# More products of zeros, the first loads at once, and a new order of work in a fused attention and MoE kernel

## The chip, the cores and the metric

The kernel runs on one core of one Trainium2 chip. The metric is the device time of one execution in microseconds (us). TensorE (PE in the rows) multiplies matrices, VectorE (DVE) and ScalarE (ACT) do elementwise work, GpSimd (POOL) does a little of it, and SyncE (SP) issues nearly all transfers (DMA).

## The reference

Linear attention, a norm, and a two-layer network with the activation h·cos(h), all in float32:

```python
kv  = einsum('bhsd,bhse->bhde', k, v)          # 8 batches, 8 heads, 576 tokens, 64 columns
out = einsum('bhsd,bhde->bhse', q, kv)
x   = out / sqrt(mean(out*out, -1) + 1e-6) * g_norm      # heads side by side: 4608 x 512
h   = x @ w_in                                 # 512 -> 2048
y   = (h * cos(h)) @ w_out                     # 2048 -> 512
```

## The kernel before

**Tiling.** The 4608 tokens are nine chunks of 512. The width of 2048 is sixteen blocks of 128, with a weight tile `wi` and a weight tile `wo` for each. A step is one chunk and one block. Its first stage makes h in a PSUM bank, from four groups of three products of 512 columns (`xhi` with two parts of `wi`, `xlo` with one). ScalarE and VectorE make h·cos(h) from it (`ki`, `r`, then `ghi` and `glo`), and its second stage adds it onto four `acc` tiles with four groups of three products. The products of 128 x 512 are nearly all of TensorE's work.

**The front.** The first two chunks (`FRONT`) are made ready in another way than the later ones. For each of four pairs of heads p, `kv_front_part` multiplies k and v of a batch (36 small products for batch 0, 24 for batch 1), and `x_front_part` transposes q (four products with `ident`), multiplies it with kv, takes the norm, and transposes back (four products, `ident` and `r`). Their tiles are lent from buffers that later hold weights, so k, v and q of the front stand in the rows under names such as `wo` and `wi`. The last of the front's k and v are those of batch 1, p = 3.

**Weights.** They come as 64-bit words of 512 KB a tile. `w_part` turns them into two float32r parts, with some three operations on ScalarE and four on VectorE.

**The order of work.** The program holds a small planner (`Order`). Each piece of work is a generator that asks for an engine, a duration and a priority. The planner puts the pieces on the engines by its own estimates, and the instructions are issued in that order and kept in it. `due(i)` is the planned time of step i, `haste` adds a correction to the priority of single pieces (through `put_off`), and loads are pieces on a planned engine "DMA". So a changed number moves instructions on all engines. Loads of weights are issued on line 437, the front's k and v on 386 and 388, its q on 418 and 423, all from SP; the first k and v come from ScalarE's queue. Line 207 is the helper through which every compute instruction goes.

**The start.** 34 products of zeros run on TensorE while the first loads are on their way.

Of the kernel before, what the change touches and what calls it, by code (L numbers as in the profile page):

```python
# [15 lines left out]
AF = mybir.ActivationFunctionType  # L16
# [35 lines left out]
class Order:  # L52
# [23 lines left out]
    def advance(self, proc, value):  # L76
        while True:
            try:
                req = proc.gen.send(value)
            except StopIteration:  # L80
                self.live.discard(proc)
                return
            value = None
            self.seq += 1
            if req[0] == "run":
                proc.shape = req[3] if len(req) > 3 else None
                self.pending.append((req[2], self.seq, proc.t, req[1], proc))
                return
            if req[0] == "wait":
                proc.t = max([proc.t] + [e.t for e in req[1] if e.t is not None])  # L90
                proc.left = [e for e in req[1] if e.t is None]
                if proc.left:
                    for e in proc.left:
                        e.waiters.append(proc)
                    return
            else:
                tokens = req[1]
                if not tokens.free:
                    heapq.heappush(tokens.waiters, (req[2] if len(req) > 2 else -100.0, self.seq, proc))
                    return  # L100
                t, value = heapq.heappop(tokens.free)
                proc.t = max(proc.t, t)
# [24 lines left out]
    def run(self):  # L127
        while self.pending:
# [15 lines left out]
            if e == "PE":  # L144

                d = (2 * d if start < 6 else d) + (self.CHANGE if proc.shape != self.shape else 0)
                self.shape = proc.shape
# [7 lines left out]
def tile_kernel(  # L155
# [40 lines left out]
    sched = Order()  # L196
    sched.busy["DMA"] = 1.0

# [40 lines left out]
    bank = ps_s.tile([P, 512], F32, name="bank0")  # L239
    for _ in range(34):  # L240
        pe.matmul(out=bank[:, 0:P], lhsT=zeros, rhs=zeros, start=True, stop=True)
    ident = const.tile([P, P], F32, name="ident")
# [26 lines left out]
    def due(i):  # L269
# [4 lines left out]
    haste = {  # L274
        ("load kv", 0, 0): -15.1, ("load kv", 0, 1): 6.2, ("load kv", 0, 2): 2.5, ("load kv", 0, 3): 3.5,
        ("load kv", 1, 1): -98.4, ("load kv", 1, 3): 27.5, ("load q", 0, 0): -4.0, ("load q", 0, 1): -28.8,
        ("load q", 0, 3): -16.6, ("load q", 1, 0): -10.5, ("load q", 1, 2): 10.0, ("load q", 1, 3): -24.8,
        ("load", "wi", 3): 10.0, ("load", "wo", 0): 10.0, ("load", "wo", 1): -130.0, ("load", "wo", 2): -13.1,
        ("kv", 0, 1): -13.1, ("kv", 0, 3): -10.0, ("x", 1, 0): -90.9, ("x", 1, 1): -5.1, ("x", 1, 2): -20.0,
        ("x", 1, 3): 11.8, ("wi", 1): 10.0, ("wi", 12): 8.7, ("wi", 13): 5.0, ("wi", 7): -10, ("wi", 9): -5,  # L280
        ("wo", 0): -46.3, ("wo", 12): 19.2, ("wo", 13): 59.3, ("wo", 2): 10.6, ("wo", 4): 10.6, ("wo", 5): -7.5,
        ("wo", 8): 14.1, ("h", 10): -14.4, ("h", 11): 75.5, ("h", 13): 6.2, ("h", 15): -21.9, ("h", 23): 16.3,
        ("h", 26): -21.2, ("h", 31): 25.1, ("h", 36): 54.9, ("h", 4): 10, ("act", 11): -46.1, ("act", 13): 15.3,
        ("act", 16): 16.2, ("act", 29): 32.0, ("act", 35): 63.7, ("act", 4): -10, ("act", 5): -8.1,
        ("act", 8): 10.6, ("acc", 0): 28.7, ("acc", 1): 19.9, ("acc", 10): 20.7, ("acc", 13): 59.2,
        ("acc", 14): 44.4, ("acc", 18): 32.3, ("acc", 26): 10.6, ("acc", 28): 15.6, ("acc", 33): 25.2,
        ("acc", 46): 5.6, ("acc", 53): 6.8, ("acc", 8): 12.3, ("xd", 2, 0): -3.8, ("xd", 2, 2): -11.8,
        ("xd", 2, 3): -24.5, ("xd", 3, 0): -12.5,
    }
# [31 lines left out]
    kv_split = {(b, p): Event() for b in range(FRONT) if max(chunks_of(b)) >= FRONT for p in range(NP)}  # L321
    g_in, over_in = Event(), events(B)
    w_done = {key: Event() for key in need}
# [26 lines left out]

    def load_g():
        pass

    def g_part():
        yield "wait", [g_in]
        yield "run", [("ACT", 0.1)], -11.0
        act.copy(out=gcol[D:2 * D, :], in_=gcol[0:D, :])

    def two(shape, dtype, which):
# [16 lines left out]
    def kv_loads_front(b, p, tags):  # L376

        def issue():
            shape = [P, 2, SQ, D] if b else [P, SF, D]
            kv_tiles[b, p] = [wpool.tile(shape, F32, name=f"{kind}{j}") for kind, j in tags]  # L380
            for t, src in zip(kv_tiles[b, p], (k, v)):
                heads = src[b, 2 * p:2 * p + 2]

                queue = nc.sync if b or p else act
                if b:
                    queue.dma_start(out=t[0:SP], in_=heads.rearrange("h (p i) d -> p h i d", i=SQ))  # L386
                else:
                    queue.dma_start(out=t, in_=heads.rearrange("h (p i) d -> (h p) i d", i=SF))
            if not b and not p:
                act.activation(out=warm, in_=warm, func=AF.Sin)  # L390
                act.dma_start(out=gcol[0:D, :], in_=g_norm.rearrange("(d o) -> d o", o=1))
        return issue
# [59 lines left out]
    def kv_front_part(b, p, prio):  # L452
# [13 lines left out]
        sched.fire(kv_used[b, p], end)  # L466
        done = [Event(), Event()]

        def copies(j):
# [61 lines left out]
    def x_front_part(c, p, prio):  # L531
# [5 lines left out]
        qn = q_tiles.pop((c, p)).rearrange("p j (m s) d -> p (j m) (s d)", s=2)  # L537
        ps_t = ps_tile(bank)
        for n in range(NTT):
            pe.transpose(out=ps_t[:, n * P:(n + 1) * P], in_=qn[:, n, :], identity=ident)  # L540
# [4 lines left out]
        give_ps(bank, end)  # L545
        todo = front_rows(c)
        yield "wait", [kv_done[b, p] for b in {b for b, _, _, _ in todo}]
        acc = (p + 2) % NTT
# [22 lines left out]
        def heads(t):  # L571
# [7 lines left out]
        dve.tensor_scalar(out=ms, in0=ms, scalar1=EPS, scalar2=None, op0=ALU.add)  # L579
        yield "run", [("POOL", 1.4)], prio  # L580
        rinv = small.tile([P, 2 * NTT], F32, name="rinv")
# [5 lines left out]
            out=heads(x), in0=heads(ps[:, 0:CH]),  # L587
            in1=rinv.rearrange("p (n o) -> p n o", o=1).broadcast_to([P, 2 * NTT, D]), op=ALU.mult)
        _, end = yield "run", [("PE", 0.5)], prio
        for a in range(NTT):  # L590
# [20 lines left out]
    def x_part(c, p, prio):  # L611
# [20 lines left out]
        for j in range(2):  # L632
            yield "take", t_psa, prio
            banks.append((yield "take", t_bank, prio))
        _, end = yield "run", [("PE", sum(2 * max(0.11, (n + 32) / 2400) for _, _, _, n in parts))], -1.0
        both = [ps_tile(bank) for bank in banks]
# [61 lines left out]
    def w_part(key, prio):  # L698
# [22 lines left out]
        act.activation(out=w32, in_=words(F32, 1), func=AF.Copy, scale=HW_SCALE)  # L721
        yield "wait", [low_done]
        yield "run", [("DVE", 0.69)], prio
        wi = w32.bitcast(I32)
# [52 lines left out]
    def act_part(i, h, bank):  # L777
# [10 lines left out]
        dve.scalar_tensor_tensor(out=r, in0=ki, scalar=-C2, in1=r, op0=ALU.mult, op1=ALU.add)  # L788
        sched.give(t_ki, end)

        yield "run", [("ACT", act_us())], prio
# [21 lines left out]
    def stage2_part():  # L813
        for i, (c, j, first, final) in enumerate(steps):
            yield "wait", [w_done["wo", j], g_done[i]]
            for t in range(NTT):
# [13 lines left out]
                if final:  # L830
                    sched.spawn(out_part(c, t, accs[t], j == NJ - 1, due(i + 3)), end + 0.1)
            sched.give(t_g, end)
# [63 lines left out]
    for b in range(FRONT):  # L896
        used = [q_used[c, p] for c in range(FRONT) if c >= b for p in range(NP)]
        used += [e for (x, _), e in kv_split.items() if x == b]
        [(kind, j)] = lend(1, used, -1)
        kv_front.append(wpool.tile([P, H, P], F32, name=f"{kind}{j}"))  # L900
        (pool if b else dve).memset(kv_front[b], 0.0)
    for c in range(FRONT):
        for p in range(NP):
            t = due(begin[c]) - 32 + 3 * p if c else -100.0 + p
            t += put_off("load kv", c, p)
            load(2.4 if c else 1.9, t, [kv_in[c, p]], kv_loads_front(c, p, lend(2, [kv_used[c, p]])))
            if p in (0, 2):
                [key] = lend(1, [q_used[c, p], q_used[c, p + 1]])
            t += put_off("load q", c, p)
            load(1.1 if c else 0.85, t, [q_in[c, p]], q_loads_front(c, p, key))  # L910
            if c == 0 and p == 1:
                load(0.5, t, [g_in], load_g)
                sched.spawn(g_part())
    for c in range(FRONT):
# [4 lines left out]
    for key in sorted(need, key=lambda x: (need[x], x)):  # L919
        t = due(need[key]) - 14.0 + put_off("load", *key)  # L920
        load(1.5, t, [w_in[key]], w_loads(key), wait=lent.get(key, ()))
        sched.spawn(w_part(key, due(need[key]) - 0.0 + put_off(*key)))
# [58 lines left out]
```

## Time and profile before

| | |
|---|---|
| time, median of 3 runs | 860.48 us (859.9 to 860.79) |
| the profiled execution | 862.48 us, its span 860.7 us |
| TensorE busy | 850.8 us, 99% of the span |
| VectorE, ScalarE busy | 651.4 and 556.7 us |
| moved by DMA | 59.52 MB |

The span runs from the first to the last instruction, and the profiled execution's time is 1.78 us longer than its span. A product's row is its time in the pipeline, so that rows overlap.

### The profile page before, as it was taken

Reading aid. Unit: us, or ns where it says so; the run is one execution under the profiler, and the core shown is the slowest. Engines: PE = TensorE matmul, PEld = TensorE weight load, DVE = VectorE, ACT = ScalarE, POOL = GpSimd, SP = SyncE. Lnnn points to the kernel's source line nnn. Section 1 sums busy time; section 2 is a strip of 40 time slices with the busy share of each in tenths; the row PEclk is TensorE's granted clock in tenths of the full one; section 3 lists DMA queues with packets and bytes.
Section 4 is the critical chain, followed back from the end, with each engine's and each line's share of the span. In section 5 each row is a group of like instructions: output and inputs, shape, how many; then the busy total and the mean of one; then the engine's idle time right before and its main releaser. Section 6 shows DMA issues by size and latency. Waiting matters only on the chain.

```text
span 860.7 us, 12112 instructions
## 1 busy us (share of the span) xinstructions
PE 850.8 (99%) x4458; PEld 705.5 (82%) x4458; DVE 651.4 (76%) x1053; ACT 556.7 (65%) x1059; POOL 103.7 (12%) x49
## 2 busy tenths in 40 slices
PE   8899999999999999999999999999999999999998
PEld 7688888888788888888888888888888888888886
DVE  4999988899987757886778667876778678864554
ACT  4788888667666556665666566756666666664443
POOL 3310000013122101111102101210111111110000
PEclk9999999999999999999999999999999999999999
DMA  8996020371403111400223020402000110010001
GB/s 298 265 398 201 2 85 25 108 199 25 111 13 97 26 62 22 113 13 13 65 52 82 1 74 12 115 9 62 13 13 13 47 28 1 1 38 12 1 0 50
DMA packets 104731, 59.52 MB, mean 69 GB/s; under 512 B 69728, under 2 KB 95072, under 8 KB 104672
## 3 DMA queue, kind: packets, MB, share of 16 engines
q1 hardware_dynamic: 104160, 58.02, 23.4%
q8 instruction: 35, 0.57, 0.3%
q10 hardware_dynamic: 512, 0.72, 0.2%
q14 instruction: 24, 0.20, 0.1%
HBM read 47.19 MB, written 11.53 MB: 68 GB/s over the span
## 4 chain that ended last, share of the span: by engine, by line
PE 95%; DMA 3%; SPq 1%; DVE 0%; issue 0%; ACT 0%; DVEq 0%
PE bank L207 50%; PE acc L207 45%; DMA wi<-in_v_dram 2%; DMA wo<-in_k_dram 1%; DVE r L207 0%; SPq L437 0%; SPq L386 0%; SPq L418 0%; ACT r L207 0%; DVE glo L207 0%; DVE slot L207 0%; ACT ki L207 0%; ACT slot L207 0%; DVEq L207 0%
## 5 line engine op out<-in xcount | busy, mean ns | idle before, releaser
L207 PE MATMUL acc<-wo,ghi 128*128 128x512 f32 x1152 | 355.7, 390 | 0.0
L207 PE MATMUL bank<-xhi,wi 128*128 128x512 f32 x1088 | 337.3, 391 | 0.1
L207 PEld LDWEIGHTS acc<-wo,ghi 128*128 128x128 f32 x1152 | 215.7, 188 | 45.2 <-DVE slot L207 0.4
L207 ACT ACTIVATE r<-r 128x512 f32<-128x512 f32 x288 | 181.3, 630 | 94.4 <-DVE r L207 92.0
L207 PEld LDWEIGHTS bank<-xhi,wi 128*128 128x128 f32 x1088 | 202.4, 188 | 41.6 <-DVE wi L207 0.4
L207 PE MATMUL acc<-wo,glo 128*128 128x512 f32 x576 | 224.5, 390 | 0.3 <-DVE glo L207 0.3
L207 PE MATMUL bank<-xlo,wi 128*128 128x512 f32 x544 | 212.1, 390 | 0.1
L207 POOL TENSOR_TENSOR rinv<-ms,mhalf 128x16 f32<-128x16 f32 (+1 forms) x36 | 99.2, 2756 | 651.5 <-DVE ms L207 651.5
L207 DVE SCALAR_TENSOR_TENSOR r<-ki,bank 128x512 f32<-128x512 int32 x144 | 98.7, 686 | 72.1 <-ACT ki L207 70.6
L207 ACT ACTIVATE ki<-bank 128x512 int32<-128x512 f32 x144 | 85.6, 595 | 90.3 <-PE bank L207 86.5
L207 DVE SCALAR_TENSOR_TENSOR r<-r,bank 128x512 f32<-128x512 f32 x144 | 98.3, 683 | 55.1 <-ACT r L207 54.4
L207 PEld LDWEIGHTS acc<-wo,glo 128*128 128x128 f32 x576 | 108.1, 188 | 23.3 <-DVE glo L207 0.7
L207 PEld LDWEIGHTS bank<-xlo,wi 128*128 128x128 f32 x544 | 102.1, 188 | 21.8 <-DVE xlo L207 0.6
L207 ACT CAST ghi<-r 128x512 fp32r<-128x512 f32 x144 | 89.1, 619 | 43.2 <-DVE r L207 40.8
L207 DVE TENSOR_TENSOR glo<-r,ghi 128x512 fp32r<-128x512 f32 x144 | 99.0, 688 | 23.6 <-ACT ghi L207 21.2
L207 DVE SCALAR_TENSOR_TENSOR r<-ki,r 128x512 f32<-128x512 int32 x144 | 98.6, 685 | 1.2
L207 DVE TENSOR_TENSOR slot<-bank,slot 64x512 f32<-64x512 f32 x56 | 38.5, 688 | 19.0 <-ACT slot L207 18.1
L207 ACT COPY slot<-bank 64x512 f32<-64x512 f32 x56 | 32.6, 581 | 21.1 <-PE bank L207 20.2
L207 ACT ACTIVATE slot<-acc 128x512 f32<-128x512 f32 (+1 forms) x39 | 22.5, 592 | 8.8 <-PE acc L207 7.6
L207 ACT COPY swp<-part 32x16 f32<-32x16 f32 x112 | 22.6, 202 | 7.5 <-DVE part L207 5.8
L207 DVE STREAM_TRANSPOSE slot<-rinv 128x512 f32<-128x512 f32 x28 | 19.8, 706 | 4.1 <-POOL rinv L207 4.0
L207 DVE SCALAR_TENSOR_TENSOR sg<-sg,m 128x512 int32<-128x512 int32 x32 | 21.7, 685 | 0.6 <-ACT sg L207 0.6
(94 smaller groups left out, 580.1 us busy)
## 6 DMA issues: line engine op xcount, KB each, us to landing
out_dram<-slot SPq DMA_DIRECT2D x35, 256.0 KB, 2.0
wo<-in_moe_w_out_dram SPq DMA_DIRECT2D x16, 512.0 KB, 8.4
wi<-in_moe_w_in_dram SPq DMA_DIRECT2D x16, 512.0 KB, 8.6
m<-in_k_dram SPq DMA_DIRECT2D x24, 256.0 KB, 3.8
sg<-in_v_dram SPq DMA_DIRECT2D x24, 256.0 KB, 4.4
part<-slot SPq DMA_DIRECT2D x8, 256.0 KB, 5.7
slot<-part SPq DMA_DIRECT2D x8, 256.0 KB, 3.5
qb<-in_q_dram SPq DMA_DIRECT2D x32, 48.0 KB, 2.3
```

The costliest lines, as they stand in the source:

```text
L207: return lambda *a, **kw: tc.keep_in_program_order(f(*a, **kw))
```

## The change

- 40 products of zeros at the start instead of 34, and 14 more in `x_front_part`, ahead of the transposes of the second pair of q.
- The first k and v and the first two q are issued at once, ahead of all planned loads. The load of `g_norm` moves behind them and becomes two loads, which replace a copy on ScalarE.
- The planner's numbers: the DMA begins at 4.5 instead of 1.0, TensorE at 5.5, loads and the power of the norm on GpSimd have other durations, and TensorE's work before 6.0 is no longer planned at double length.
- `haste` has more entries and other values, with further places where it is added.

```diff
-    sched.busy["DMA"] = 1.0
+    sched.busy["DMA"] = 4.5
...
-    for _ in range(34):
-        pe.matmul(out=bank[:, 0:P], lhsT=zeros, rhs=zeros, start=True, stop=True)
+    def warm_up(ps, n):
+        for _ in range(n):
+            pe.matmul(out=ps[:, 0:P], lhsT=zeros, rhs=zeros, start=True, stop=True)
+
+    warm_up(bank, 40)
+    sched.busy["PE"] = 5.5
...
-                d = (2 * d if start < 6 else d) + (self.CHANGE if proc.shape != self.shape else 0)
+                d += self.CHANGE if proc.shape != self.shape else 0
...
-        ("load kv", 0, 0): -15.1, ("load kv", 0, 1): 6.2, ("load kv", 0, 2): 2.5, ("load kv", 0, 3): 3.5,
+        ("load kv", 0, 0): -15.1, ("load kv", 0, 1): 6.2, ("load kv", 0, 2): -615.2, ("load kv", 0, 3): 6.1,
...
+        if c == 0 and p == 1:
+
+            warm_up(ps_t, 14)
...
-        yield "run", [("POOL", 1.4)], prio
+        yield "run", [("POOL", 1.65)], prio
...
+    at_once = {("kv", 0, 0): 6.8, ("q", 0, 0): 5.2, ("q", 0, 1): 6.8}
...
-            load(2.4 if c else 1.9, t, [kv_in[c, p]], kv_loads_front(c, p, lend(2, [kv_used[c, p]])))
+            issue = kv_loads_front(c, p, lend(2, [kv_used[c, p]]))
+            if ("kv", c, p) in at_once:
+                issue()
+                sched.fire(kv_in[c, p], at_once["kv", c, p])
+            else:
+                load(2.5 if c else 1.5, t, [kv_in[c, p]], issue)
...
-        load(1.5, t, [w_in[key]], w_loads(key), wait=lent.get(key, ()))
+        load(1.5 if need[key] < 5 else 1.3, t, [w_in[key]], w_loads(key), wait=lent.get(key, ()))
```

On TensorE, at the start, before: `ident` with `wi` is a transposition of q, `wo` with `wi` of 64 columns are the front's k and v, `acc` from `wo` and `m` is q times kv.

```order
68 L207 MATMUL bank_84<-zeros 128x128
69 L207 MATMUL bank_146<-ident,wi_137 128x128 x4
70 L207 MATMUL bank_156<-ident,wi_137 128x128 x4
71 L207 MATMUL bank_165<-wo_141,wi_140 64x64 x18
72 L207 MATMUL bank_188<-ident,wi_154 128x128 x4
73 L207 MATMUL acc_199<-wo_133,m 128x2x64 x4
74 L207 MATMUL bank_218<-wi_185,wo_184 64x64 x18
75 L207 MATMUL bank_243<-ident,wi_154 128x128 x4
76 L207 MATMUL acc_263<-wo_133,m 128x2x64 x4
77 L207 MATMUL bank_270<-wo_210,wi_209 64x64 x18
78 L207 MATMUL bank_293<-wo_239,wo_238 64x64 x18
```

The same place of the change, with the rows of zeros between left out:

```order
81 L209 MATMUL bank_157<-ident,wi_147 128x128 x4
82 L209 MATMUL bank_168<-wo_144,wi_143 64x64 x18
83 L209 MATMUL bank_187<-wi_154,wo_153 64x64 x18
84 L209 LDWEIGHTS zeros
85 L209 MATMUL bank_212<-zeros 128x128
...
112 L209 MATMUL bank_212<-ident,wi_147 128x128 x4
113 L209 MATMUL acc_238<-wo_139,m 128x2x64 x4
114 L209 MATMUL bank_251<-ident,wi_162 128x128 x4
115 L209 MATMUL acc_269<-wo_139,m 128x2x64 x4
116 L209 MATMUL bank_284<-ident,wi_162 128x128 x4
117 L209 MATMUL bank_292<-wo_244,wo_243 64x64 x18
```

Two pairs of k and v now come ahead of the second transposition of q, the pair of p = 2 moves into second place, and the 14 products of zeros stand behind it.

On SP, the first loads, before:

```order
1 L418 DMA wi_137<-in_q_dram 128x2x256 x2
2 L418 DMA wi_154<-in_q_dram 128x2x256
3 L437 DMA wo_161<-in_moe_w_out_dram 128x512
4 L388 DMA wo_184<-in_k_dram 128x576
5 L388 DMA wi_185<-in_v_dram 128x576
6 L418 DMA wi_154<-in_q_dram 128x2x256
7 L388 DMA wi_209<-in_k_dram 128x576
```

And of the change:

```order
1 L425 DMA wi_147<-in_q_dram 128x2x256 x2
2 L398 DMA wo_153<-in_k_dram 128x576
3 L398 DMA wi_154<-in_v_dram 128x576
4 L425 DMA wi_162<-in_q_dram 128x2x256
5 L444 DMA wi_166<-in_moe_w_in_dram 128x4x128
6 L444 DMA wo_210<-in_moe_w_out_dram 128x512
7 L425 DMA wi_162<-in_q_dram 128x2x256
8 L398 DMA wo_243<-in_k_dram 128x576
```

The second k and v come ahead of the third q and of the first weight tile, and a `wi` tile is now among the first eight loads; before, the first `wi` is row 16.

On SP, up to the last k and v of the front (`96x2x384`, batch 1), before:

```order
26 L386 DMA wi_468<-in_v_dram 96x2x384
27 L423 DMA wo_491<-in_q_dram 96x2x128
28 L423 DMA wo_491<-in_q_dram 128x2x128
29 L423 DMA wo_491<-in_q_dram 32x2x128
30 L437 DMA wo_506<-in_moe_w_out_dram 128x512
31 L423 DMA wo_491<-in_q_dram 96x2x128
32 L423 DMA wo_491<-in_q_dram 128x2x128
33 L423 DMA wo_491<-in_q_dram 32x2x128
34 L437 DMA wi_541<-in_moe_w_in_dram 128x4x128
35 L437 DMA wo_566<-in_moe_w_out_dram 128x512
36 L386 DMA wi_579<-in_k_dram 96x2x384
37 L386 DMA wo_580<-in_v_dram 96x2x384
```

And of the change:

```order
28 L444 DMA wo_478<-in_moe_w_out_dram 128x512
29 L396 DMA wo_502<-in_k_dram 96x2x384
30 L396 DMA wi_503<-in_v_dram 96x2x384
31 L444 DMA wi_531<-in_moe_w_in_dram 128x4x128
32 L444 DMA wo_544<-in_moe_w_out_dram 128x512
33 L444 DMA wi_567<-in_moe_w_in_dram 128x4x128
34 L430 DMA wo_467<-in_q_dram 96x2x128
35 L430 DMA wo_467<-in_q_dram 128x2x128
36 L430 DMA wo_467<-in_q_dram 32x2x128
37 L444 DMA wi_601<-in_moe_w_in_dram 128x4x128
38 L396 DMA wi_612<-in_k_dram 96x2x384
39 L396 DMA wo_613<-in_v_dram 96x2x384
```

Ten weight tiles are now issued ahead of the last k and v of the front; before it was eight.

## Rows read from the trace of the kernel before

**Rows 1.** The page: the chain that ended last, shares of the span.

```profile
PE 95%; DMA 3%; SPq 1%; DVE 0%; issue 0%; ACT 0%; DVEq 0%
```

**Rows 2.** Stretches: length, busy PE, PEld, DVE, ACT, POOL, clock, DMA share, GB/s.

```profile
5.00:57.00 52.00, 47.26 (x460) 38.88 (x461) 40.85 (x79) 36.33 (x80) 14.36 (x9) 1.00 1.01 325
```

**Rows 3.** The same view, other stretches.

```profile
12.50:17.50 5.00, 3.49 (x74) 3.07 (x72) 4.32 (x10) 1.71 (x5) 1.66 (x1) 1.00 1.10 328
17.50:20.00 2.50, 2.50 (x53) 2.43 (x49) 1.16 (x5) 1.93 (x7) 1.64 (x1) 1.00 0.70 176
20.00:27.50 7.50, 6.37 (x82) 5.44 (x81) 7.02 (x14) 6.18 (x14) 3.24 (x2) 1.00 1.03 316
27.50:32.00 4.50, 3.97 (x28) 2.41 (x24) 4.48 (x10) 3.51 (x10) 1.10 (x1) 1.00 1.05 239
32.00:35.00 3.00, 2.56 (x34) 2.25 (x35) 2.68 (x6) 2.05 (x7) 0.96 (x1) 1.00 0.56 128
35.00:42.00 7.00, 6.60 (x36) 5.09 (x34) 6.55 (x13) 5.33 (x11) 1.64 (x1) 1.00 1.07 295
45.00:57.00 12.00, 12.00 (x70) 9.88 (x70) 11.23 (x21) 9.80 (x18) 3.89 (x2) 1.00 1.05 398
57.00:200.00 143.00, 143.00 (x705) 118.75 (x704) 128.02 (x210) 113.27 (x209) 2.90 (x1) 1.00 0.37 114
200.00:855.00 655.00, 654.74 (x3256) 543.03 (x3255) 480.34 (x761) 404.06 (x767) 82.16 (x27) 1.00 0.14 37
```

**Rows 4.** TensorE in order of time: start, length, what, idle time before it.

```profile
0.98 3.81 PE L207 MATMUL bank<-zeros 128*128 128x128 bf16 x34 [0.98 <-DVE zeros L207]
5.28 1.08 PE L207 MATMUL bank<-ident,wi 128*128 128x128 f32 x4 [0.48 <-POOL wo L207]
6.75 1.12 PE L207 MATMUL bank<-ident,wi 128*128 128x128 f32 x4 [0.39 <-DMA wi<-in_q_dram]
7.79 2.19 PE L207 MATMUL bank<-wo,wi 64*64 64x64 f32 x36
9.91 0.85 PE L207 MATMUL bank<-ident,wi 128*128 128x128 f32 x4
...
11.87 1.26 PE L207 MATMUL bank<-wi,wo 64*64 64x64 f32 x36
13.07 0.66 PE L207 MATMUL bank<-ident,wi 128*128 128x128 f32 x4
15.23 1.16 PE L207 MATMUL acc<-wo,m 128*128 128x128 f32 x8 [1.51 <-DVE m L207]
...
24.44 0.63 PE L207 MATMUL acc<-ident,r 128*128 128x128 f32 x4 [1.13 <-DVE r L207]
...
32.44 0.92 PE L207 MATMUL bank<-wi,wo 96*64 96x64 f32 x24 [0.75 <-DMA wi<-in_v_dram]
...
42.07 0.92 PE L207 MATMUL bank<-wo,wi 96*64 96x64 f32 x24 [0.47 <-issue]
```

**Rows 5.** The chain that ended last, 9 to 33 us: start, length, what.

```profile
9.28 8.24 DMA wi<-in_v_dram
...
17.54 0.39 SPq L437
...
20.53 11.77 DMA wi<-in_v_dram
32.30 0.14 issue
```

**Rows 6.** DMA issues, 32 to 46 us: count, KB each, median us to landing.

```profile
wi<-in_k_dram SPq DMA_DIRECT2D x1, 288.0 KB, 7.8
wo<-in_v_dram SPq DMA_DIRECT2D x1, 288.0 KB, 8.2
```

**Rows 7.** SP in order of time, from 32 us: start, length, what.

```profile
32.32 0.39 SPq L437 DMA_DIRECT2D wi<-in_moe_w_in_dram  x1
...
33.79 0.45 SPq L386 DMA_DIRECT2D wo<-in_v_dram  x1
```

## What the change should do to the time

> **What bounds the kernel now.** I read the chain that ended last first: 95% of it is TensorE, 3% are transfers [rows 1]. Then I looked for the places where TensorE stands idle, stretch by stretch. From 57 to 200 us it is busy for 143.00 of 143.00, and from 200 to 855 us for 654.74 of 655.00 [rows 3]. So past the front there is 0.26 us to win, and the work there is the same products before and after. From 5 to 57 us it is busy for 47.26 of 52.00, idle for 4.74 [rows 2]. All that this change can win lies in that stretch. Two things are to be seen there.
>
> First, the idle time: 0.39 us for a q, 1.51 and 1.13 us for VectorE, 0.75 us for a v, and 0.47 us ahead of the last small products of the front at 42.07 [rows 4]. The last one is marked "issue", but the v of that pair was issued at 33.79 and took 8.2 us [rows 6, 7], so it landed at 41.99. That wait is for a transfer too. Behind 42.07 there is no wait left in the front.
>
> Second, slow products. Four transpositions take 1.08 and 1.12 us at 5.28 and 6.75, 0.85 at 9.91 and 0.66 at 13.07; 36 small products take 2.19 us at 7.79 and 1.26 at 11.87 [rows 4]. The granted clock reads 1.00 in every stretch [rows 2, 3], but by these durations TensorE is at the lower of its two levels (1.2 GHz) up to some point near 10 us, and at 2.4 GHz behind it.
>
> The transfers are the other half. The chain goes through loads up to 32.30 [rows 5]. SP's issue at 17.54 comes right behind the landing of the load issued at 9.28 (9.28 + 8.24 = 17.52), and the one at 32.32 behind that of 20.53 [rows 5, 7]. In the order these last two are rows 26 and 34: a load waits for the one eight loads back. That leaves holes: 176 GB/s at a share of 0.70 from 17.5 to 20, and 128 GB/s at 0.56 from 32 to 35, where weights alone run at 398 [rows 3].
>
> **One point carries the sum.** I take the start of the small products on the front's last k and v, 42.07 us before. I counted TensorE's rows ahead of it in both orders: they are the same set (the same transpositions, products of k and v, of q and kv, and three whole steps of the first stage), but for 20 more products of zeros. So whatever the reordering does ahead of this point, what counts is when it is reached. It needs TensorE's own work to be through, and it needs the last load.
>
> **TensorE's side.** The 6 further zeros at the start cost nothing: 34 took 3.81 us, 0.112 each [rows 4], so 40 end near 5.4 us, where TensorE stood idle for 0.48 us before the first transposition anyway. If this gap gone lets the clock rise before the front's first k and v, the slow time goes: 0.42 + 0.46 + 0.19 for the transpositions against 0.66, and 0.93 for the 36 products, 2.0 us. The trace does not show the moment without the gap, so the bounds are 0 and 2.0. The 14 zeros stand in TensorE's path: 1.57 us at 0.112, or 0.9 if they quicken as the small products do (2.19 to 1.26). The waits for transfers (0.39 + 0.75 + 0.47 = 1.61 us) can all go; those for VectorE (1.51 + 1.13) I leave, since the same copies and norms stand ahead of the same products. TensorE's own side is then ready at 42.07 - 2.0 - 1.61 + 0.9 = 39.4 at best, and at 42.07 - 1.61 + 1.57 = 42.0 if the clock rises as late as before.
>
> **The loads' side.** Issuing the first loads at once takes no bytes away, and the second k and v now come in place of a weight tile of 512 KB. In the whole of SP's order ten weight tiles stand ahead of the last v, not eight. So 2 x 512 KB, 1.05 MB, are added. From 12.5 to 42 us the core moved 328 x 5 + 176 x 2.5 + 316 x 7.5 + 239 x 4.5 + 128 x 3 + 295 x 7 = 7,975 KB [rows 3]; now it must move 9.02 MB. Bounds: if only the two holes close, 0.30 x 2.5 + 0.44 x 3 = 2.07 us go and 1.05 / 0.398 = 2.63 come, so the last v lands at 42.0 + 0.56 = 42.6. If all went at the rate of the weights alone, it would be 12.5 + 9.02 / 0.398 = 35.2. I take 316 GB/s, the rate of 20 to 27.5 us, because there the same mixture of front loads and weights runs with no hole (share 1.03), and eight loads back there is now a larger one still under way: 12.5 + 9.02 / 0.316 = 41.0.
>
> That is later than 39.4. So the loads end last, and the point moves from 42.07 to about 41.1, with the 0.08 us from landing to product.
>
> The Trainium skill speaks against a gain here. "DMA: Bandwidth & Descriptors", section "Issuing engines are not separate DMA queues", says that DMAs interleave on the same 16 engines whoever starts them, and that issuing them side by side saves only issue time. The rows agree where the share stands at 1.03 to 1.10 [rows 3], and not in the holes, which are issue waiting for a landing; by the rule alone the point would stay at 42.1 or later.
>
> **The other edits.** The loads of g_norm (256 bytes each) and the copy that falls away lie beside the loads; uncovered, the copy would be some 0.2 us of ScalarE. GpSimd's 1.65 in place of 1.4 is a number of the planner and adds no instruction. Behind the point I count 0.2 of the 0.26 us as won, and the new order of the later steps as nothing, because VectorE has 15 of 143 us free from 57 to 200 [rows 3]. If a chain there comes late, its price is of the size of the 1.51 us above.
>
> **Sum.** -1.0 - 0.2 = -1.2 us. The profiled execution is 862.48 us, 1.78 more than its span, and would become 861.3. It is 2.0 us above the median of 860.48, so against the median I forecast 859.3.
>
> **Rivals.**
> - *The loads are in time.* For it: much of the front's slow rate (239 GB/s from 27.5 to 32, at a share of 1.05) may come from which loads meet, and the order of these is new. TensorE's side decides: 39.4, -2.7 - 0.2, 857.6 us.
> - *The loads come late, slower than before.* For it: 1.05 MB more ahead of the last v. If the holes stay, it lands at 42.0 + 2.6 = 44.6, and the time is 863.0. It decides from a landing past 43.8. Against it: the loads that SP waits for now have weight tiles behind them.
> - *The change does nothing.* The clock rises as late as before, or earlier with no use because the last v lands at 42 again: 860.4. The Trainium skill has this too: "TensorE: Matmul & The Clock Gate", section "What's actually happening", warns that the number of slow products differs from run to run and is not to be fitted. No run here shows it yet.
> - *A new wait in the later steps.* One VectorE chain late by 1.5 us turns -1.2 into +0.3: 860.8; two of them, 862.3.
>
> **How the numbers follow.** The forecast, loads last at 40.3 to 42.2, has 0.38, with a range of its own of 858.4 to 860.5. Loads in time: 0.34. Nothing: 0.12. Late loads: 0.09. New wait: 0.07. About 0.2%, 1.7 us, is what a measurement of this kernel can tell from no change. Faster by more than that (below 858.8) are nearly all of the second case, 0.32, and the quick end of the first, 0.06: 0.38. Slower (above 862.2) are most of the late loads and the second half of the new waits: 0.10. The rest is 0.52. The range of 857.2 to 861.5 leaves out the slowest of the late loads and the ends.
>
> **What would show it.** In the changed trace, zeros and the first transposition join without the gap of 0.48 us, and the 36 first products take nearer 1.3 than 2.2 us. The stretch from 17.5 to 35 us has no slice at a share of 0.6 or 0.7. The last 24 small products of the front start near 41.1, directly behind a landing. If they start near 39.5 with no wait for a transfer, the first rival is right; past 43, the second. From 57 us on TensorE's idle time stays below 0.3 us. The prediction falls if TensorE's idle time ahead of that point, now 4.7 us, does not shrink, or if idle time turns up behind it.

## The result: slower by 0.4%

The changed kernel takes 863.94 us, median of 5 runs (863.31 to 866.33), beside 860.79 for the kernel before (859.9 to 861.74): ratio 1.004, 95% interval 1.0023 to 1.0057. A second profile with its own 6 runs gave the same, 1.004 (1.0027 to 1.0054). The profiled execution took 863.6 us, its span 861.8.

The changed kernel, stretches as in [rows 2, 3]; columns: length, busy PE, PEld, DVE, ACT, POOL, clock, DMA share, GB/s:

```profile
5.00:57.00 52.00, 45.34 (x468) 36.83 (x466) 40.70 (x78) 38.95 (x86) 15.40 (x9) 1.00 1.02 338
17.50:20.00 2.50, 1.65 (x42) 1.53 (x40) 0.74 (x3) 1.09 (x6) 2.01 (x1) 1.00 1.12 314
20.00:27.50 7.50, 6.90 (x71) 5.71 (x69) 6.91 (x15) 6.81 (x16) 3.67 (x2) 1.00 0.99 282
32.00:35.00 3.00, 2.28 (x24) 1.60 (x26) 2.73 (x6) 1.73 (x4) 1.13 (x1) 1.00 1.05 381
35.00:42.00 7.00, 7.00 (x52) 5.75 (x47) 6.66 (x14) 6.44 (x15) 1.09 (x1) 1.00 1.10 302
57.00:200.00 143.00, 143.00 (x706) 118.70 (x705) 126.11 (x207) 111.90 (x207) 2.90 (x1) 1.00 0.37 109
200.00:855.00 655.00, 655.00 (x3260) 543.80 (x3259) 481.76 (x762) 403.76 (x765) 80.55 (x27) 1.00 0.14 37
...
0.00:12.50 12.50, 9.84 (x142) 9.34 (x143) 2.36 (x7) 3.57 (x9) 4.51 (x13) 1.00 0.78 270
6.00:8.00 2.00, 1.52 (x38) 1.17 (x36) 0.00 (x0) 1.00 (x3) 0.00 (x0) 1.00 0.56 159
...
0.00:43.28 43.28, 36.01 (x410) 29.92 (x411) 29.08 (x58) 28.80 (x64) 16.10 (x19) 1.00 0.97 303
```

The two holes of [rows 3] at 17.5 and 32 us are not there (shares 1.12 and 1.05), and behind 57 us TensorE has no idle time left (0.26 us before). Yet from 5 to 57 us it is idle for 6.66 us; it was 4.74. And there is a new hole from 6 to 8 us, at a share of 0.56.

TensorE of the changed kernel in order of time, beside [rows 4]:

```profile
0.98 4.45 PE L209 MATMUL bank<-zeros 128*128 128x128 bf16 x40 [0.98 <-DVE zeros L209]
5.22 1.06 PE L209 MATMUL bank<-ident,wi 128*128 128x128 f32 x4
6.21 1.31 PE L209 MATMUL bank<-wo,wi 64*64 64x64 f32 x36
9.20 1.26 PE L209 MATMUL bank<-wi,wo 64*64 64x64 f32 x36 [1.68 <-DMA wi<-in_v_dram]
10.39 0.95 PE L209 MATMUL bank<-zeros 128*128 128x128 bf16 x14
...
16.31 1.26 PE L209 MATMUL bank<-wo,wo 64*64 64x64 f32 x36 [0.70 <-DMA wo<-in_v_dram]
18.43 1.26 PE L209 MATMUL bank<-wo,wi 64*64 64x64 f32 x36 [0.85 <-DMA wo<-in_v_dram]
...
43.28 0.92 PE L209 MATMUL bank<-wo,wi 96*64 96x64 f32 x24
```

And the chain that ended last in it (start, length, what), where [rows 5] showed loads up to 32.30:

```profile
2.23 6.83 DMA wi<-in_v_dram
...
9.45 8.84 DMA wo<-in_v_dram
...
18.43 1.28 PE bank L209 x36
...
31.19 1.95 POOL rinv L209
...
33.16 0.70 DVE r L209
...
33.91 9.33 PE bank L209 x68
...
43.28 0.93 PE bank L209 x24
```

The last 24 small products start at 43.28, not at 41.1. No wait stands directly ahead of them, though their v landed only just in time, at 43.1 (issue on SP, and the row of its landing):

```profile
34.64 0.32 SPq L396 DMA_DIRECT2D wo<-in_v_dram  x1
...
wo<-in_v_dram SPq DMA_DIRECT2D x1, 288.0 KB, 8.5
```

The chain goes back, through 24.85 us of the front's own work and norms, to the *fourth* v of batch 0, which was issued at 9.45 and landed at 18.29. In the kernel before nobody waited for that v.

**The profile of before was of a slow start.** A second profile of the unchanged kernel before has this on TensorE:

```profile
5.04 0.95 PE L207 MATMUL bank<-ident,wi 128*128 128x128 f32 x4 [0.25 <-DMA wi<-in_q_dram]
6.32 0.66 PE L207 MATMUL bank<-ident,wi 128*128 128x128 f32 x4 [0.33 <-DMA wi<-in_q_dram]
6.91 1.26 PE L207 MATMUL bank<-wo,wi 64*64 64x64 f32 x36
...
16.39 1.22 PE L207 MATMUL bank<-wo,wo 64*64 64x64 f32 x36
...
41.03 0.92 PE L207 MATMUL bank<-wo,wi 96*64 96x64 f32 x24 [0.50 <-issue]
```

The 36 first products take 1.26 instead of 2.19 us, and the point that the prediction rests on is at 41.03 instead of 42.07. Its span is 859.7 us, and up to 12.5 us it moved 298 GB/s where the change moves 270:

```profile
0.00:12.50 12.50, 10.21 (x130) 8.82 (x130) 3.52 (x8) 4.82 (x10) 4.50 (x13) 1.00 0.84 298
5.00:57.00 52.00, 46.80 (x464) 38.40 (x465) 41.89 (x81) 37.08 (x82) 14.34 (x9) 1.00 1.04 321
17.50:20.00 2.50, 2.50 (x26) 2.46 (x23) 1.78 (x5) 1.69 (x4) 1.14 (x1) 1.00 1.01 282
32.00:35.00 3.00, 3.00 (x29) 2.62 (x24) 3.00 (x6) 2.50 (x8) 0.00 (x0) 1.00 0.82 248
```

From 5 to 57 us it is idle for 5.20 us. And of the two holes of [rows 3] only the second is in it, so the first was of one execution too.

Against this profile the change loses 2.04 us up to the fourth pair of k and v (16.39 to 18.43), 2.25 us up to the last pair, and 2.1 us at the end: the whole loss is there by 18.4 us.

### The profile page after: what moved, and what is told of

Read it like the earlier page. It is cut to its first block, busy times and chain, and to the rows that moved or that the text cites. A ratio compares the mean times of both kernels' runs of the same rounds, so it can differ in the third digit from the quotient of the medians.

```text
span 861.8 us, 12170 instructions
## 1 busy us (share of the span) xinstructions
PE 850.4 (99%) x4478; PEld 705.5 (82%) x4478; DVE 651.1 (76%) x1050; ACT 557.7 (65%) x1061; POOL 103.1 (12%) x49
## 4 chain that ended last, share of the span: by engine, by line
PE 96%; DMA 2%; DVE 1%; POOL 1%; SPq 0%; issue 0%; ACT 0%; POOLq 0%
PE bank L209 50%; PE acc L209 46%; DMA wo<-in_v_dram 1%; DMA wi<-in_v_dram 1%; POOL rinv L209 1%; DVE r L209 0%; DVE ms L209 0%; DVE wi L209 0%; DVE sg L209 0%; DVE wo L209 0%; ACT wo L209 0%; SPq L425 0%; SPq L398 0%; DVE xlo L209 0%; DVE slot L209 0%
## 5 line engine op out<-in xcount | busy, mean ns | idle before, releaser
L209 DVE TENSOR_TENSOR slot<-bank,slot 64x512 f32<-64x512 f32 x56 | 38.5, 688 | 19.2 <-ACT slot L209 18.4
L209 ACT COPY slot<-bank 64x512 f32<-64x512 f32 x56 | 32.6, 583 | 20.4 <-PE bank L209 18.4
L209 DVE TENSOR_TENSOR m<-qT,m 64x512 fp32r<-64x512 f32 x28 | 19.2, 685 | 4.7 <-ACT m L209 4.0
```

The source lines that it names most:

```text
L209: return lambda *a, **kw: tc.keep_in_program_order(f(*a, **kw))
```

## The experiments

The theories in the expectations: **1** or **F**, TensorE's instruction fetch (a transfer of its own, see the last section) holds one DMA engine back; **2** or **H**, the first loads (the two small loads of g_norm, the hole at 6 to 8 us); **3** or **L**, the order of the loads, with the loss at the start or at the end of the front; **4** or **Z**, the zeros' own time. Each ratio is to the kernel before on the same chip, with its 95% interval; the changed kernel stands at 1.0040.

**Both kernels once more.**

> The kernel before, unchanged, profiled a second time. Its first profiled execution was 862.48 us, 1.7 us above the median of 860.79, and the changed kernel's was 863.6, 0.3 below its median of 863.94. So the two profiles differ by 1.1 us and the medians by 3.15. If the first profile of before was of a usual execution, the second reads within 0.3 us of it in its front: four transpositions at 1.1 us each up to 10 us, TensorE idle for 4.7 us from 5 to 57 us, and the last 24 small products of the front at 42.0. If it was a slow one (the moment at which the short rows begin differs from execution to execution), the second has a front that is up to 2 us shorter: 36 first products at 1.3 instead of 2.19 us and the last small products at 40 to 41. Ratio of the times 1.000.

Measured: 860.82 us, ratio 0.999 (0.998 to 1.0). The first profile was of a slow start (above).

> The changed kernel, unchanged, profiled a second time: 863.5 to 865 us, fetch of TensorE's instructions at 12.5 to 13.3 us, the fourth k and v of batch 0 start at 18 to 19 us, the last 24 small products of the front at 43 to 45.

Measured: 864.31 us, 1.004 (1.0027 to 1.0054); span 861.7, last small products at 43.18 as in the first profile, here behind a wait of 0.37 us for the last v.

**The zeros.** The change without its 14 zeros; with its old 34 and without the 14; and the kernel before with all 54.

```diff
 # no14; order_only also has warm_up(bank, 34)
-        if c == 0 and p == 1:
-            warm_up(ps_t, 14)
```

> The changed kernel without the 14 products of zeros in the second place. Theory 1 (TensorE's instruction fetch, a transfer of 16 KB after every 256 or so of its instructions, comes earlier because of the added zeros and the faster start, and holds one of the 16 DMA engines back by about 2 us while the first k and v of the front are on their way): 28 instructions less put the fetch from 13.0 to about 15 us; the loads that land last on that engine before then gain up to 1 us; 0.5 to 1.5 us faster than the changed kernel. Theory 2 (the two small loads of g_norm and the places they hold delay the second k and v): the hole from 5.5 to 8.25 us stays, 0 to 0.3 us faster. Theory 3 (two more weight tiles ahead of the last k and v): no change in the last landing, 0 to 0.3 us. Theory 4 (the zeros' own time on TensorE): the 0.8 us of the zeros go, and 0.8 us at the end with them, unless a wait for a transfer takes their place.

Measured: 864.89 us, 1.0038 (1.0026 to 1.005). Nothing is won: the waits for the third and fourth v grow from 0.70 and 0.85 to 1.63 and 1.32 us.

> The changed kernel with 34 products of zeros at the start and without the 14: the new order, the first loads and the numbers of the planner alone. Theory L (order of the loads): as slow as the changed kernel, 863 to 865 us. Theory Z (the zeros' own time): 1.2 to 1.6 us faster than the changed kernel, 862.4 us or less.

Measured: 863.72 us, 1.0039 (1.0024 to 1.0054). The new order, with the loads at once and the planner's numbers, is the whole loss. In this profile the granted clock read 0.50 from 10 to 12.5 us, and yet the last small products start at 43.42, nearly as in the change: slower rows of TensorE at this place cost next to nothing.

```profile
9.02 2.03 PE L209 MATMUL bank<-wi,wo 64*64 64x64 f32 x36 [1.82 <-DMA wi<-in_v_dram]
```

```diff
 # zeros_only, in the kernel before
-    for _ in range(34):
+    for _ in range(40):
...
+        if c == 0 and p == 3:
+            for _ in range(14):
+                pe.matmul(out=ps_t[:, 0:P], lhsT=zeros, rhs=zeros, start=True, stop=True)
```

> The kernel before with the 40 and 14 products of zeros and nothing else of the change; the 14 stand ahead of its third transposition of q, behind the first products of k and v. Theory L (the new order of the loads makes the front late, and the zeros lie in time in which TensorE waits for loads anyway): the second profile of before has waits for a v of 0.74 us at 31.38 and 0.50 at 41.03 behind that place, which take the 0.95 us of the 14 zeros up; 0 to 0.4 us slower than before. Theory Z (the zeros' own time, 0.64 + 0.95 us on TensorE, is the loss): 1.2 to 1.6 us slower than before, with the last 24 small products of the front near 42.4. Theory 1 (TensorE's instruction fetch comes earlier behind more zeros and holds one DMA engine back): fetch at 13 instead of 15 us and the third and fourth k and v late, 1 us or more slower.

Measured: 861.64 us, 1.0008 (0.9998 to 1.0017): not to be told from no change. The interval reaches 1.5 us and so doesn't rule theory 4 out by itself; with order_only, which has the loss without the zeros, it falls. Theory 1 falls in part: the fetch came at 11.99 and the last part of each load was some 2 us late from there on, but this order had time to spare, and the third and fourth products started at 15.50 and 16.60 with no wait.

**The instruction fetch and the small loads.**

```diff
 # wide
-    warm_up(bank, 40)
+    wide = zeros.rearrange("p (o f) -> p o f", o=1).broadcast_to([P, 4, P])
+    for _ in range(10):
+        pe.matmul(out=bank.rearrange("p (o f) -> p o f", o=4), lhsT=zeros, rhs=wide, start=True, stop=True)
 # gpool
-        act.dma_start(out=gcol[j * D:(j + 1) * D, :], in_=g_norm.rearrange("(d o) -> d o", o=1))
+        pool.dma_start(out=gcol[j * D:(j + 1) * D, :], in_=g_norm.rearrange("(d o) -> d o", o=1))
 # narrow (narrow_gpool: narrow and gpool; before_narrow: 68 of them in the kernel before)
+    for _ in range(80):
+        pe.matmul(out=bank[0:64, 0:64], lhsT=zeros[:, 0:64], rhs=zeros[:, 0:64], start=True, stop=True)
```

> The changed kernel with 10 products of zeros of 512 columns at the start in place of 40 of 128 columns: the same columns and about the same time on TensorE, but 60 instructions less. Theory 1 (TensorE's instruction fetch holds one DMA engine back): the fetch that now comes at 13.0 us moves behind 16 us; the fourth v of batch 0 lands whole near 16.5 instead of 18.3, and its products start near 17 instead of 19; 1 to 1.5 us faster at the end. Theories 2 to 4 (small loads of g_norm; two more weight tiles; the 14 zeros' own time): all of these stay, so no change, within 0.3 us.

Measured: 864.35 us, 1.0036 (1.0023 to 1.0048). The fetch stayed at 13.23, so this tells nothing of theory 1.

> The changed kernel with the two loads of g_norm issued from GpSimd instead of ScalarE, so that they don't stand between the first loads. Theory 2 (they hold two of the eight places for loads and one engine with packets of 4 bytes): the second v lands near 8.1 instead of 9.06, the hole from 5.5 to 8.25 us is gone, TensorE's wait of 1.68 us at 9.20 shrinks to 0.7, and the end comes 0.7 to 1.5 us earlier. Theory 1 (instruction fetch): the third and fourth v still land at 16.2 and 18.3, so what is won at 9.2 is lost again at 16.3 and 18.4: 0 to 0.3 us. Theories 3 and 4 (two more weight tiles; the 14 zeros' own time): 0 to 0.3 us.

Measured: 865.23 us, 1.0049 (1.0031 to 1.0067). The second v was in time (products at 7.61 instead of 9.20), but the fourth pair started at 17.99 and the last at 43.47. The hole was not closed, it moved:

```profile
0.00:12.50 12.50, 10.31 (x147) 9.73 (x147) 3.42 (x9) 5.15 (x12) 5.67 (x15) 1.00 0.77 271
6.00:8.00 2.00, 1.68 (x50) 1.58 (x51) 0.21 (x1) 1.00 (x3) 0.40 (x1) 1.00 1.04 360
10.00:12.50 2.50, 1.61 (x15) 1.37 (x13) 1.35 (x3) 2.26 (x5) 0.00 (x0) 1.00 0.70 238
```

From 6 to 8 us it moves 360 instead of 159 GB/s, from 10 to 12.5 only 238, and up to 12.5 us the mean is 271 beside 270. Theory 2 falls as the cause of the time.

> The changed kernel with 80 products of zeros of 64 x 64 at the start in place of 40 of 128 x 128: about the same columns, 80 more instructions on TensorE ahead of the first loads. Theory F (the instruction fetch holds one DMA engine back just as the third and fourth k and v are carried): the fetch is asked for earlier and falls at 7 to 10 us, into or near the hole in the transfers, where the engine can catch up; the fourth v lands whole near 16.5 instead of 18.3, TensorE's waits of 0.70 and 0.85 us at 16.31 and 18.43 fall below 0.5 in sum, 1 to 1.5 us faster than the changed kernel. Theory H (the hole and the bytes ahead are what makes them late): no change, 863.5 to 865 us. If the fetch stays near 13 us, nothing is told.

Measured: 863.64 us, 1.0033 (1.0021 to 1.0046). The fetch came at 10.59, the lag began there and stayed, and the fourth v landed at 18.29 as in the change. So the moment of the fetch is not the cause either.

> The same with the loads of g_norm issued from GpSimd, which closes the hole at 5.5 to 8.25 us. Theory F: as narrow, with up to 0.5 us more. Theory H: 0.5 to 1.5 us faster than narrow. If both are needed, this one alone comes down to 861.5 us or less.

Measured: 866.99 us, 1.0071 (1.0056 to 1.0086). The fourth pair starts 1.08 us earlier, and the end is later: now the last v is waited for.

```profile
17.35 1.26 PE L209 MATMUL bank<-wo,wi 64*64 64x64 f32 x36 [0.93 <-DMA wo<-in_v_dram]
...
44.89 1.35 PE L209 MATMUL bank<-wo,wi 96*64 96x64 f32 x24 [2.06 <-DMA wo<-in_v_dram]
```

> The kernel before with 68 products of zeros of 64 x 64 at the start in place of 34 of 128 x 128. Theory F: the fetch comes at 8 to 11 instead of 15 us and the lag with it; in this order the products on the third and fourth k and v have time to spare, so 0 to 1 us slower, as with the 54 zeros (fetch at 12.0, +0.7 us). Theory H: no change, within 0.3 us.

Measured: 861.1 us, 1.0004 (0.9993 to 1.0015): nothing, with the fetch at 10.0.

**The order of the loads, moved.** Each moves loads on SP alone; the other engines keep their order.

```diff
 # hoist_first and hoist_last: the k and v of AHEAD[key] are issued just ahead of weight tile key
+    AHEAD = {("wi", 0): [(0, 1), (0, 3)]}   # hoist_last: {("wi", 3): [(1, 3)]}
...
             kind, j = key
+            for pair in AHEAD.get(key, ()):
+                early[pair]()
 # before_wi0 and before_two, in the kernel before: weight tiles issued just ahead of a k and v
+    AHEAD = {(0, 3): [("wi", 0)]}           # before_two: {(1, 3): [("wi", 4), ("wi", 5)]}
```

> The changed kernel with the k and v of batch 0, p = 1 and 3, issued ahead of the first two weight tiles and the last q instead of behind them (1.3 MB less ahead of them); all engines but SP keep their order. Theory L, lost at the start (two weight tiles ahead of the third and fourth k and v): TensorE's waits for a v of 0.70 us at 16.31 and 0.85 at 18.43 go, the fourth v lands near 15 instead of 18.3; 1 to 2 us faster than the changed kernel if the weight tiles that now come later are still in time. Theory L, lost at the end (two more weight tiles ahead of the last k and v): the same waits go, but the last 24 small products stay at 43: 0 to 0.4 us.

Measured: 873.17 us, 1.0146 (1.0129 to 1.0162), a miss of both theories. The k and v were in time, but ScalarE converts the first weight tile ahead of a copy of the front, in an order that is kept: TensorE waited 4.12 us at 16.82 and 4.68 us at 40.93, and its granted clock read 0.81 from 13 to 20 us.

> The changed kernel with the last k and v of the front issued two weight tiles and a q earlier, so that eight weight tiles stand ahead of it as before; all engines but SP keep their order. Theory L, lost at the end (the prediction's term: two more tiles at 316 GB/s, that is 3.3 us of the last landing): the last v lands 3 us or more earlier, the last 24 small products of the front start at 41 to 42 instead of 43.28, and the time falls by 1 us or more. Theory L, lost at the start: in the profile of the changed kernel TensorE reaches these products without a wait (busy from 34.9 to 43.28), so an earlier landing gives 0 to 0.3 us.

Measured: 865.77 us, 1.0047 (1.0034 to 1.006). The last v was no longer waited for, and it didn't help; a weight tile that had been pushed back took its place in the chain. In this profile the fourth pair, too, started late, at 19.48 instead of 18.43.

```profile
45.25 0.92 PE L209 MATMUL bank<-wo,wi 96*64 96x64 f32 x24 [0.74 <-ACT m L209]
...
32.31 10.70 DMA wi<-in_moe_w_in_dram
...
43.02 0.66 ACT sg L209
```

> The kernel before with one load moved: the first wi tile (512 KB) is issued ahead of the third and fourth k and v of batch 0, about where the change has it, instead of behind the first k and v of batch 1. All other engines keep their order. Theory L, lost at the start: these k and v land 1.3 us later or, with one DMA engine held back, up to 3 us later; TensorE waits ahead of its products at 15.29 and 16.39, where the second profile of before shows no wait; 0.5 to 2 us slower than before. Theory L, lost at the end: within 0.3 us of before.

Measured: 861.4 us, 0.9995 (0.9982 to 1.0007). A wait of 0.44 us at 16.44 and one of 1.30 for the last v at 41.60, and the time the same: one tile earlier cost nothing in the old order.

> The kernel before with two loads moved: two weight tiles of 512 KB are issued ahead of the last k and v of the front, so that ten weight tiles stand ahead of them as in the change instead of eight. All other engines keep their order. Theory L, lost at the end (the prediction's term): 1.05 MB at 316 to 398 GB/s, 2.6 to 3.3 us later; TensorE's wait of 0.50 us at 41.03 grows to 3 us or more, and the kernel is 2.5 to 3.5 us slower than before. Theory L, lost at the start: the tiles ahead of the last k and v matter only as far as TensorE's other work doesn't cover them, which in this order of before is not at all; so the same slowdown here, with no waits at 16 to 19 us such as the change has.

Measured: 866.19 us, 1.0044 (1.0029 to 1.0059). The profile is of the slowest of its 12 executions (868.33).

```profile
33.20 1.55 PE L207 MATMUL bank<-wi,wo 96*64 96x64 f32 x24 [2.20 <-DMA wi<-in_v_dram]
...
46.42 1.25 PE L207 MATMUL bank<-wo,wi 96*64 96x64 f32 x24 [2.52 <-DMA wo<-in_v_dram]
```

Only the second wait stands behind the two moved tiles, which were issued at 34.06. The v of the first was issued ahead of them, at 22.75 (20.20 in the second profile of before), behind an issue on SP that took 2.47 us. So two tiles ahead of the last k and v cost 0.44% here, as much as the change costs, but how much of the 5.4 us at the point (46.42 beside 41.03) is theirs is not shown.

**Fewer bytes, order kept.**

```diff
 # lean_first: keys wi 0, wo 1; lean_last: wi 3, wi 4; the rest of each tile is set to 0 at the start
-            nc.sync.dma_start(out=t, in_=src)
+            n = 1 if key in lean else NP
+            nc.sync.dma_start(out=t[:, 0:n], in_=src[:, 0:n])
```

> The changed kernel that loads only a quarter of its first two weight tiles (the rest is set to zero by GpSimd at the start, so that those columns of the weights are left out): 786 KB less ahead of the k and v of batch 0, p = 1 and 3, with every engine's order as it is. Theory L, lost at the start: these k and v land about 2 us earlier (786 KB at 400 GB/s), TensorE's waits of 1.68 us at 9.20, 0.70 at 16.31 and 0.85 at 18.43 shrink to 1.5 us or less in sum, the last 24 small products start at 41 to 42 instead of 43.28, and the time falls to 861 to 862.5 us. Theory L, lost at the end: the waits go there too, but the last 24 small products stay near 43 and the time at 863 or more.

Measured: 861.66 us, 0.9995 (0.9983 to 1.0008): the whole loss is gone, with every engine in the new order. So that order costs by its loads. No run takes the same bytes out of the old order; that these two tiles are what the new order put in the way is therefore not shown.

```profile
15.01 1.26 PE L209 MATMUL bank<-wo,wo 64*64 64x64 f32 x36
16.11 1.22 PE L209 MATMUL bank<-wo,wi 64*64 64x64 f32 x36
...
41.33 0.92 PE L209 MATMUL bank<-wo,wi 96*64 96x64 f32 x24 [0.45 <-DMA wo<-in_v_dram]
```

> The changed kernel that loads only a quarter of the two weight tiles that stand last ahead of the last k and v of the front (the rest set to zero at the start, these columns of the weights left out): 786 KB less there, every engine's order as it is. Theory L, lost at the end: the last v lands 2 us or more earlier and the time falls by 1 us or more. Theory L, lost at the start: TensorE is not waiting for it, 0 to 0.3 us.

Measured: 863.75 us, 1.0022 (1.001 to 1.0034). The last v landed at 41.4, and the last small products start at 43.19, with no wait, as in the change:

```profile
43.19 0.92 PE L209 MATMUL bank<-wo,wi 96*64 96x64 f32 x24
```

The fourth pair started at 18.46, as in the change too. Whether the rest of the difference to 1.0040 is real is unclear; the intervals overlap.

> lean_first (a quarter of the first two weight tiles, the rest set to zero) without the 14 products of zeros. If the zeros lie in TensorE's path as soon as the loads are in time: 0.7 to 1 us faster than lean_first, with the fourth pair of batch 0 near 15.2 instead of 16.1. If the loads still end last there (lean_first waited 0.45 us for the last v): less than 0.5 us, the last 24 small products at 40.9 or later behind a wait for the last v of 1 us or more.

Measured: 862.32 us, 1.0006 (0.9995 to 1.0017). The 14 zeros cost nothing even here: the last v was waited for 0.93 us at 41.63.

> narrow_gpool and lean_last in one kernel: 80 narrow products of zeros, the loads of g_norm from GpSimd, and only a quarter of the two weight tiles that stand last ahead of the last k and v (the rest set to zero, these columns of the weights left out). Two bounds that end together: the fourth pair of batch 0 starts near 17.4 as in narrow_gpool, no wait for the last v, the last 24 small products at 42 to 42.5 instead of 43.2 to 44.9, and the time 1 us or more below the changed kernel and 3 us or more below narrow_gpool. One bound (the last v, or another wait that follows): 863.5 us or more.

Measured: 865.55 us, 1.0038 (1.0023 to 1.0053), the second of the two cases. The fourth pair started at 16.13, and at 26 us TensorE was 2.3 us ahead of the change. The last part of the fourth v came 0.2 us behind the 14th of its 16, against 2.1 in the change, so the lag was gone here as well, with nothing won at the end. Then ScalarE waited for a weight tile, with the front's copy and VectorE's norm behind its conversion, and TensorE slowed down:

```profile
24.67 5.53 DMA wo<-in_moe_w_out_dram
30.23 0.03 ACT sg L209
...
32.82 13.19 PE bank L209 x88
```

So in these runs the front has not two bounds but several of nearly the same date: whichever was relieved, the next was close behind.

## Why the prediction was wrong, point by point

- **The gap and the slow products.** Right as far as they go. Zeros and first transposition join, and the 36 first products take 1.31 instead of 2.19 us. But the second profile of before has them at 1.26: most of this gain was of one execution, not of the kernel. The Trainium skill had the warning that the prediction quotes ("TensorE: Matmul & The Clock Gate", "What's actually happening": the number of slow products differs from run to run); two profiles of one kernel now show it. So the point to start from was 41.03, and the forecast of 41.1 meant no gain.
- **The waits for transfers "can all go".** The three (0.39, 0.75, 0.47) went, and three others came, of 1.68, 0.70 and 0.85 us, 3.23 in sum. The sum had them at nothing, and TensorE's own side was ready at 43.24 instead of 39.4 to 42.0.
- **The 14 zeros, 0.9 us.** The row says 0.95. At the end they cost nothing that shows (no14, order_only, lean_first_no14), and waits for loads stand on either side of them.
- **The loads' side: here the prediction failed.** The last v landed at 43.1 where the sum had 41.0. The rate was right. Up to 43.28 us the change moved 303 x 43.28 = 13.11 MB, up to 12.5 us 270 x 12.5 = 3.38; that is 9.74 MB in 30.78 us, 316 GB/s, the number that the prediction took. What was wrong are the 9.02 MB that had to move by then, by 0.72 MB, or 2.3 us. One half of that (0.35 MB) is that it took the stretch before 12.5 us as unchanged: the profiles of before moved 298 x 12.5 = 3.73 MB there. "Issuing the first loads at once takes no bytes away", but SP then waits for landings between 4 and 12 us, in a hole that gpool could only shift. The Trainium skill's rule that the prediction weighed and set aside for the holes ("DMA: Bandwidth & Descriptors", "Issuing engines are not separate DMA queues": issuing side by side saves only issue time) fits here: the loads at once brought 270 GB/s beside 298, so no gain. The other half (0.37 MB) is what is left over; that these are bytes of later loads, which share the stretch, is argued and not shown.
- **"What counts is when the point is reached, and it needs the last load."** That the last v alone carries the sum was wrong too. In the change two things came at nearly the same moment: the last v (43.1) and TensorE itself (43.24), whose chain goes back to the fourth v of batch 0. The last v freed alone won nothing at the point (43.19 in lean_last, 45.25 in hoist_last), and neither did a fourth v that came earlier alone (43.47 in gpool, 44.89 in narrow_gpool). With 786 KB less ahead of both (lean_first), the point came 1.95 us earlier; at 316 GB/s that is worth up to 2.5 us. So not one load carries the sum; several do, and the new order made them late together.
- **The rivals.** "The loads come late, slower than before" had 0.09 and came nearest, with 863.0 us by its sum and 863.94 measured. In six later profiles of the changed order (after_again, order_only, narrow, no14, narrow_gpool, wide) the last v was waited for, and the point came at 43.2 to 46.4. But part of that is luck: its reason, that the holes stay and the last v lands at 44.6, was not what happened in the change. The argument against it (SP's waits now have weight tiles behind them) held for the two holes and overlooked the new one. No new wait came in the later steps, and the 0.26 us behind 57 us were won.

What stays open: the two profiled executions of the change lie 0.3 and 0.8 us below their medians and the second one of before 0.6 above its, so that some 1 us of the 3 us between the medians is in no profile. Which part of the new order makes the loads late (the tiles further ahead, the hole from 6 to 8 us, or both) was not taken apart by a run that has one without the other and is as fast as before. And what moves the fetch of instructions was not found.

## What to carry to other kernels

Profile the unchanged kernel twice before a sum rests on the first microseconds of one execution. In a start that is bound by loads, count the bytes from the first load to the point, in both orders and from time zero: products of zeros moved, shrunk or removed there were worth nothing here, and relieving one load showed the next. Where engines keep a planned order, moving a load alone is dangerous (hoist_first, +1.5%), because a conversion that waits for it holds all that is queued behind it.

## What the runs showed of the hardware

**TensorE's instructions are fetched by DMA while the loads run.** The change's transfers from 12 to 14.5 us, by queue (packets, MB, share):

```profile
q1 hardware_dynamic: 548, 0.99, 104.0%
q8 instruction: 1, 0.02, 2.4%
```

That one packet has 16,384 bytes and took 0.95 us. A load lands in 16 parts; from the records of packets and landings (us):

```
kernel         fetch at   last part behind the 14th: load before, load after
before_again   15.04      0.5   0.9
after          13.03      0.1   1.5
zeros_only     11.99      0.2   1.9
narrow         10.59      0.2   1.5
before_wi0     14.09      0.2   1.0
```

In these profiles the last part of the loads falls behind around the fetch, by 0.4 to 1.7 us, and in the change it stays 1.5 to 2.3 us behind until 25 us. That the fetch takes the time of one DMA engine fits this, but no record names the engine, and in before_again a load that landed at 14.87, ahead of the fetch, was already 0.9 us behind. A load is as late as its last part: 14 parts of the change's fourth v were in at 16.23, the last at 18.29, and its products started at 18.43.

**A wait can cost the clock.** In before_two, behind waits of 2.20 and 2.52 us, 24 small products took 1.55 and 1.25 us instead of 0.92, and the granted clock read 0.87 from 30 to 57 us. So it did in the same stretch of both, behind a wait of 1.58. Rows at that length are those of the lower level (1.2 GHz). In order_only 36 products took 2.03 us instead of 1.26 behind a wait of 1.82, and in narrow_gpool the last 24 took 1.35 behind 2.06. Behind 1.68 us in the change and 1.88 in wide the rows stayed quick. So a wait can cost more than its own length, and part of what before_two and both lost is of this kind.
